# A decode block with cached attention: from the ninth K tile on, K loads move one V tile ahead, and value products, output weights and gather move half a step back

## The chip, the cores and the metric

The kernel runs on one NeuronCore of a Trainium2 chip. The metric is device microseconds of one execution. Of three runs of the kernel before, the median is 398.58 us (398.21 to 400.56). The profile is one further execution of the same program.

## The reference: what is computed

Eight tokens (B = 8, one per sequence, D = 512) go through an attention part and an MLP part, each behind a layer norm that is modulated by a conditioning vector `c`. All is float32. Cut to what matters:

```python
mod = (silu(c) @ w_mod).reshape(8, 6, 1, 512)          # sa, ca, ga, sb, cb, gb
h = layernorm(x) * (1 + ca) + sa
q = (h @ wq)                                            # 32 query heads of 128, 8 KV heads
k, v = k_cache[:, :, -2048:], v_cache[:, :, -2048:]     # of 8192 cached positions
o = softmax(q @ k.T * 128 ** -0.5) @ v
x = x + ga * (o @ wo)                                   # wo: 4096 x 512
h = layernorm(x) * (1 + cb) + sb
x = x + gb * (square(relu(h @ w1 + b1)) @ w2 + b2)      # 512 -> 1792 -> 512
```

For 8 sequences and 8 KV heads a window of 2048 positions by 128 numbers is read from the K cache and from the V cache, 67 MB each. Each number is used for four query heads only, so the kernel is a stream of 165 MB from HBM, with transposes and small matmuls beside it.

## The kernel before, in words

**Tiles.** A K tile K0 to K15 is one KV head for four of the sequences, 4 MiB, loaded as [128 partitions, 8192 numbers]. Two K tiles make one KV head (called a group here, g or `hk`, 0 to 7). A V tile V0 to V31 is one KV head for two sequences, 2 MiB; four V tiles make one group. K tiles lie in two "big" slots of SBUF, V tiles and other weights in five "small" slots (lines 19 and 20). The output weights `wo` come in three 2 MiB pieces, wo0 to wo2, each for two groups, in small slots; the piece for the last two groups comes with a part of `w1` into a big slot (called the tail load), the rest of `w1` into a small slot, and `w2` into the other big slot.

**Loads.** The list `loads` (lines 143 to 152) is a fixed order. `pump` (line 155) issues from its front as long as a slot of the right size is free in the order of the program; `done` (line 160) gives a slot back and calls `pump`. All loads go through SyncE's queue (SP) from lines 108 and 113, in the order of the list: where a load has to wait until PE has read the slot's last tile, everything behind it on SP waits too. The transfers then run one after another on the 16 DMA engines.

**Steps.** The work on TensorE is a loop of 38 steps, `s` (lines 500 to 539), in the order in which it is written (`manual_schedule`). A step takes half a K tile. Its parts are:

- `transposes` (line 220): 128x128 transposes of K on PE into PSUM (L231), copied out by ACT and DVE (L233); four calls a step. The last call of a K tile gives its slot back.
- `scores` (line 346): four matmuls of 512 columns (L357), two calls a step.
- `weighted(v, h)` (line 440): the value product of half a V tile, four matmuls of 512 columns (L449). Half 0 opens a PSUM tile and half 1 closes it; half 1 gives the V slot back, and four DVE operations (L463, L465) reduce the PSUM tile into `o_sb`. V tile v stands in step v + PV_LAG, where PV_LAG = 5: five steps behind the K tile's half with the same number.
- once a group, the softmax: `soft_a` (copy of the scores by ACT, L367, row maximum by DVE, L369), `soft_b` (transpose of the maxima, L374, and their maximum over the parts of a row, L377 and L383), `soft_c` (back into a column, L394 and L398, the exponential on ACT, L401, a copy by DVE, L409), `soft_d` (eight transposes of the probabilities, L425, two masked copies by DVE into `pT`, L428, and one matmul for the sums, L434).
- once a group, `gather` (line 469: one matmul, L473, and DVE's L477 and L478) and `project_o` (line 483: four matmuls with `wo`, L489, which give the `wo` slot back after each second group).

In the kernel before, both halves of V tile v stand in step v + 5, half 0 in the middle and half 1 at the end; `gather` stands in the middle of a group's second step ahead of `soft_d`, and `project_o` at the end of that step, behind `weighted(v, 1)`. In the table T is a transposes call, S a scores call, W a value product:

| step | PE's order before |
|---|---|
| first of a group | T S T W(v,0) T S [L374] T W(v,1) |
| second of a group | [L394] T S T gather soft_d W(v,0) T S T W(v,1) project_o |

After the last K tile (step 32 on) only the softmax of group 7, the last V tiles, the last `gather` and `project_o` remain, and then the MLP: `w1` (L594) and `w2` (L613), each behind a short chain on DVE. `spin` (L547) fills waits of PE with matmuls that nobody reads.

Of the kernel before, what the change touches and what calls it, by code (L numbers as in the profile page):

```python
# [20 lines left out]
def tile_adaln_cached_attention_mlp(  # L21
# [16 lines left out]
    B, HKV, SK, DH = k_cache.shape  # L38
# [9 lines left out]
    C = B // 2  # L48
    N = HKV * C
# [88 lines left out]
    def slot(key, n, o=0):  # L138

        t = slots[size_of(key)][held[key]][:, o:]  # L140
        return t[:, : t.shape[1] // n * n].rearrange("p (a n) -> p a n", n=n)

    loads = [("K", 0), *(("mod", k) for k in range(NQ)), *(("wq", k) for k in range(NQ)), ("K", 1), ("V", 0), ("K", 2)]
    for q in range(2, N // 2 + 2):
        if q > 2 and q < N // 2:
            loads.append(("K", q))
        for v in (2 * q - 4, 2 * q - 3):
            if v % (2 * C) == 2 * C - 4 and v < 6 * C:
                loads.append(("wo", v // (2 * C)))
            if v:  # L150
                loads.append(("V", v))
    loads += [("b", 0), ("tail", 0), ("w1", 0), ("w2", 0)]
    at = [0]

# [5 lines left out]
    def done(*keys):  # L160
        for k in keys:
            free[size_of(k)].append(held.pop(k))
        pump()
# [50 lines left out]
    odd = ident.rearrange("p (r u) -> p u r", u=2)  # L214
# [7 lines left out]
    def transposes(q, g, e):  # L222

        k = slot(("K", q), DH)
        if e == 0:
            KTS[q, g] = ktp.tile([P, 4, 16, 32], F32, name="kT")
        t = KTS[q, g]
        for a in range(2):
            p = ps_kt.tile([P, 4, P], F32, name="kt_ps")
            for i in range(4):  # L230
                nc.tensor.transpose(p[:, i, :], k[:, 32 * e + 16 * a + 4 * g + i, :], ident)  # L231
            i = 8 * e + 4 * a
            (nc.vector.tensor_copy if a else nc.scalar.copy)(  # L233
                t[:, :, i : i + 4, :], p.rearrange("p i (r u) -> p u i r", u=4)
            )
        if g == 3 and e == 1:
            done(("K", q))
# [89 lines left out]
    def turn_q(r):  # L327
        qs = work.tile([P, 512], F32, name="qs", tag="a", bufs=1)
        nc.scalar.copy(qs, pqs[r])
        pT_ = ps_m.tile([P, 512], F32, name="m_ps", tag="m_ps")  # L330
        for t in range(REP):
            nc.tensor.transpose(pT_[:, t * P : (t + 1) * P], qs[:, t * P : (t + 1) * P], ident)  # L332
        nc.vector.tensor_copy(  # L333
            qall[:, 4 * r : 4 * r + 4].rearrange("p g b t -> p t g b"),
            pT_.rearrange("p (t g b) -> p t g b", t=REP, g=4)[:, :, :, :B],
        )
# [28 lines left out]
    def soft_a(hk):  # L365
        ss = work.tile([P, 512], F32, name="ss", tag="a", bufs=1)
        nc.scalar.copy(ss, s_ps[0])  # L367
        mx = work.tile([P, 1], F32, name="mx")
        nc.vector.tensor_reduce(mx, ss, axis=AX.X, op=ALU.max)  # L369
        SS_[hk], MX_[hk] = ss, mx  # L370
# [21 lines left out]
    def soft_c(hk):  # L392
        pm = ps_m.tile([P, 512], F32, name="m_ps", tag="m_ps")
        nc.tensor.matmul(  # L394
            pm[:, 0:1], MX_.pop(hk).rearrange("p j r -> p (j r)"), ones[0:1, 0:1], start=True, stop=True
        )
        nm = work.tile([P, 1], F32, name="nm")
        nc.vector.tensor_copy(nm, pm[:, 0:1])  # L398
        pr = work.tile([P, 8, H, 2], F32, name="pr", bufs=1)
        z = work.tile([P, 1], F32, name="z")  # L400
        nc.scalar.activation(  # L401
            pr.rearrange("p i (r e) u -> p e i r u", e=2)[:, :, :, :, 0],
            SS_.pop(hk).rearrange("p (e i r) -> p e i r", e=2, i=8),
            AF.Exp,
            bias=nm,
            scale=SCALE,
            accum_out=z,
        )
        nc.vector.tensor_copy(pr[:, :, :, 1], pr[:, :, :, 0])  # L409
        zs = work.tile([P, B], F32, name="zs")  # L410
        nc.vector.tensor_scalar(zs, bq, z, None, op0=ALU.mult)
        P_[hk], RZP_[hk] = pr, zs
        if hk == HKV - 1:

            warm = work.tile([P, 1], F32, name="warm")
            nc.scalar.activation(warm, eps, AF.Sqrt)
# [23 lines left out]
    def weighted(n, h):  # L440

        hk, c = divmod(n, C)
        v = slot(("V", n), DH)
        if h == 0:
            O_[n] = ps_o.tile([P, 4, P], F32, name="o_ps")
        o = O_[n]
        for g in range(4):
            j = 16 * h + 4 * g
            nc.tensor.matmul(  # L449
                o[32 * g : 32 * g + 32].rearrange("p j d -> p (j d)"),  # L450
                PT_[hk][:, h, 4 * c + g].rearrange("p i r -> p (i r)"),
                v[:, j : j + 4, :].rearrange("p j d -> p (j d)"),
                start=(h == 0),
                stop=(h == 1),
            )
        if h == 0:
            return
        del O_[n]
        done(("V", n))
        if c == 0:  # L460
            OS_[hk] = work.tile([P, C, P], F32, name="o_sb", bufs=1)
        d = OS_[hk][:, c, :]
        nc.vector.tensor_scalar(d, o[:, 0, :], diag[:, 0:1], None, op0=ALU.mult)  # L463
        for j in range(1, 4):
            nc.vector.scalar_tensor_tensor(  # L465
                d, o[:, j, :], diag[:, j : j + 1], d, op0=ALU.mult, op1=ALU.add
            )

    def gather(hk):

        o = OS_.pop(hk)
        pp = ps_m.tile([P, 512], F32, name="m_ps", tag="m_ps")
        nc.tensor.matmul(  # L473
            pp, pick.rearrange("p t u -> p (t u)"), o.rearrange("p c d -> p (c d)"), start=True, stop=True
        )
        tr = work.tile([P, C, 4, 32], F32, name="tr", tag="b", bufs=1)
        nc.vector.transpose(tr, pp.rearrange("p (c d i) -> p c i d", c=C, i=4))  # L477
        nc.vector.tensor_mul(  # L478
            oT[hk % 2][:, :, :B].rearrange("p i (u c) -> p c i u", u=2),
            tr[:, :, :, :2],  # L480
            RZ_[hk].rearrange("p (u c) -> p c u", u=2)[:, :, None, :].to_broadcast([P, C, 4, 2]),
        )

    def project_o(hk):

        last = hk // 2 == HKV // 2 - 1
        w = slot(("tail", 0) if last else ("wo", hk // 2), D)
        for i in range(4):
            nc.tensor.matmul(  # L489
                wo_ps[32 * i : 32 * i + 32, :],  # L490
                oT[hk % 2][:, i, :],
                w[:, 4 * (hk % 2) + i, :],
                start=(hk == 0),
                stop=(hk == HKV - 1),
            )
        if hk % 2 and not last:
            done(("wo", hk // 2))


    for s in range(N + PV_LAG + 1):  # L500
        g, i = divmod(s, C)
        q, h = divmod(s, 2)
        v = s - PV_LAG
        soft = 1 <= g <= HKV
        if s == 1:
            turn_q(1)
        if i == 1 and soft:
            soft_c(g - 1)
        if s < N and (q, 2 * h) not in EARLY:
            transposes(q, 2 * h, 0)  # L510
        if 1 <= s <= N:
            scores((s - 1) // 2, 2 * ((s - 1) % 2) + 1)
            if i == 0:
                soft_a(g - 1)
        if s < N and (q, 2 * h) not in EARLY:
            transposes(q, 2 * h, 1)
        if v >= C and v % C == 0:
            gather(v // C - 1)
        if i == 1 and soft:
            soft_d(g - 1)  # L520
        if 0 <= v < N:
            weighted(v, 0)
        if s < N and (q, 2 * h + 1) not in EARLY:
            transposes(q, 2 * h + 1, 0)
        if s < N:
            scores(q, 2 * h)
        if s == 0:
            transposes(0, 3, 0)
            transposes(0, 3, 1)
        if i == 0 and soft:  # L530
            soft_b(g - 1)
        if s < N and (q, 2 * h + 1) not in EARLY:
            transposes(q, 2 * h + 1, 1)
        if 0 <= v < N:
            weighted(v, 1)
        if v >= C and v % C == 0:

            for hk in {N - C: (), N: (HKV - 2, HKV - 1)}.get(v, (v // C - 1,)):
                project_o(hk)


    spin_ps = ps_kt.tile([P, 4, P], F32, name="kt_ps")
# [117 lines left out]
```

## Time and profile before

| | |
|---|---|
| median of 3 runs | 398.58 us (398.21 to 400.56) |
| the profiled execution's own time | 401.07 us |
| its span, first to last instruction | 399.3 us |
| mean granted TensorE clock | 0.965 |
| HBM read | 164.77 MB, 413 GB/s over the span |
| busy | PE 334.1 us, DVE 178.5 us, ACT 97.4 us |
| K tile from issue to landing, median | 22.5 us |
| V tile from issue to landing, median | 24.9 us |

A group of the profile names line, engine, operation and `out<-in` with the tiles' names in the program; `big` and `small` are the slots. PE is the matmul side of TensorE, PEld its weight loads, SPq SyncE's queue. An idle time in square brackets stands ahead of an instruction, with what ended it. Times in a timeline or a chain are microseconds from the span's start.

### The profile page before, as it was taken

How to read it: one execution, taken by the hardware profiler on the slowest of the kernel's cores; microseconds unless marked ns; L12 is line 12 of the kernel's file. 1: busy time of each engine (PE TensorE's matmuls, PEld its weight loads, DVE VectorE, ACT ScalarE, POOL GpSimd, SP SyncE). 2: the span in 40 equal slices, each digit the busy share in tenths (PEclk: the TensorE clock that was granted, in tenths of full speed). 3: DMA queues.
4: the chain of work that ended last, by engine and by line, in shares of the span. 5: the costliest groups of instructions: out<-in, count | busy, mean ns of one | idle time of the engine just before them, and what ended most of it. 6: DMA issues, size and time to landing. Idle time of an engine off the chain costs nothing.

```text
span 399.3 us, 5987 instructions
## 1 busy us (share of the span) xinstructions
PE 334.1 (84%) x2550; PEld 165.0 (41%) x2550; DVE 178.5 (45%) x416; ACT 97.4 (24%) x169; POOL 2.5 (1%) x12
## 2 busy tenths in 40 slices
PE   1674589879998897899987988998879898997896
PEld 1430135454544443445542544454434454443124
DVE  6231024444555353644553445545552555455532
ACT  2210023342232222222321233122312222222010
POOL 2000000000000000000000000000000000000000
PEclk9996899999999998999999999999998999997899
DMA  8999999999999999999999999999999999999990
GB/s 328 418 436 428 446 416 427 435 420 442 408 430 437 435 419 432 433 418 430 422 450 410 437 422 442 415 437 415 441 414 442 418 438 420 423 428 406 433 376 26
DMA packets 10363, 165.22 MB, mean 414 GB/s; under 512 B 1112, under 2 KB 1376, under 8 KB 1632
## 3 DMA queue, kind: packets, MB, share of 16 engines
q1 hardware_dynamic: 10192, 164.71, 97.0%
q8 instruction: 20, 0.33, 0.3%
q10 hardware_dynamic: 144, 0.13, 0.1%
q14 instruction: 7, 0.06, 0.0%
HBM read 164.77 MB, written 0.07 MB: 413 GB/s over the span
## 4 chain that ended last, share of the span: by engine, by line
PE 49%; DMA 37%; DVE 9%; ACT 4%; issue 1%; SPq 0%; ACTq 0%; DVEq 0%
DMA big<-in_A_k_cache_dram 27%; PE kt_ps L231 19%; PE o_ps L449 11%; PE s_ps L357 9%; DMA small<-in_A_wq_dram 6%; DMA small<-in_w_mod_dram 4%; ACT pr L401 2%; DVE o_sb L465 2%; PE m_ps L473 2%; DVE kT L233 2%; DVE tr L477 1%; PE kt_ps L547 1%; PE m_ps L293 1%; DVE pT L428 1%; DVE pr L409 1%
## 5 line engine op out<-in xcount | busy, mean ns | idle before, releaser
L231 PE MATMUL kt_ps<-ident,big 128*128 128x128 f32 x1024 | 146.0, 285 | 30.7 <-DMA big<-in_A_k_cache_dram 20.0
L231 PEld LDWEIGHTS kt_ps<-ident,big 128*128 128x128 f32 x1024 | 112.7, 144 | 126.7 <-ACT kT L233 79.7
L233 DVE COPY kT<-kt_ps 128x512 f32<-128x512 f32 x128 | 88.3, 690 | 133.9 <-PE kt_ps L231 133.9
L233 ACT COPY kT<-kt_ps 128x512 f32<-128x512 f32 x128 | 75.0, 586 | 209.4 <-PE kt_ps L231 206.8
L357 PE MATMUL s_ps<-kT,qwin 128*32 128x512 f32 x512 | 70.1, 622 | 0.8 <-DVE qwin L343 0.8
L449 PE MATMUL o_ps<-small,pT 128*32 128x512 f32 x512 | 69.1, 620 | 0.0
L465 DVE SCALAR_TENSOR_TENSOR o_sb<-o_ps,diag,o_sb 128x128 f32<-128x128 f32 x96 | 33.7, 351 | 3.4
L318 PE MATMUL m_ps<-small,h1T 128*32 128x512 f32 x64 | 11.1, 829 | 10.3 <-DMA small<-in_A_wq_dram 10.3
L449 PEld LDWEIGHTS o_ps<-small,pT 128*32 128x32 f32 x512 | 11.4, 110 | 14.8 <-issue 13.9
L463 DVE TENSOR_SCALAR o_sb<-o_ps,diag 128x128 f32<-128x128 f32 x32 | 11.2, 351 | 13.9 <-PE o_ps L449 13.9
L357 PEld LDWEIGHTS s_ps<-kT,qwin 128*32 128x32 f32 x512 | 10.3, 109 | 12.8 <-issue 11.0
L401 ACT ACTIVATE pr<-ss,nm 128x512 f32<-128x512 f32 x8 | 9.7, 1219 | 19.1 <-DVE nm L398 19.1
L425 PE MATMUL m_ps<-ident,pr 128*128 128x128 f32 x64 | 10.5, 297 | 2.9 <-DVE tr L477 2.2
L425 PEld LDWEIGHTS m_ps<-ident,pr 128*128 128x128 f32 x64 | 7.9, 150 | 8.3 <-DVE tr L477 3.7
L473 PE MATMUL m_ps<-o_sb,pick 128*128 128x512 f32 x16 | 8.4, 604 | 3.1 <-DVE o_sb L465 1.6
L428 DVE TENSOR_TENSOR pT<-m_ps,mine 128x512 f32<-128x512 f32 x16 | 10.4, 686 | 0.4 <-PE m_ps L425 0.4
L333 DVE COPY qall<-m_ps 128x128 f32<-128x128 f32 x2 | 0.8, 390 | 21.4 <-PE m_ps L332 21.4
L318 PEld LDWEIGHTS m_ps<-small,h1T 128*32 128x32 f32 x64 | 2.1, 134 | 18.9 <-DMA small<-in_A_wq_dram 9.8
L409 DVE COPY pr<-pr 128x512 f32<-128x512 f32 x8 | 3.4, 428 | 12.1 <-ACT pr L401 12.1
L369 DVE TENSOR_REDUCE mx<-ss 128x1 f32<-128x512 f32 x8 | 5.5, 688 | 6.4 <-ACT ss L367 6.4
L293 PE MATMUL m_ps<-small,cT 128*32 128x512 f32 (+1 forms) x64 | 6.0, 492 | 2.0 <-DMA small<-in_w_mod_dram 2.0
L270 PE MATMUL m_ps<-xsum,sel 128*128 128x1 f32 x2 | 0.6, 362 | 7.9 <-DVE xsum L268 7.9
(123 smaller groups left out, 106.0 us busy)
## 6 DMA issues: line engine op xcount, KB each, us to landing
big<-in_A_k_cache_dram SPq DMA_DIRECT2D x16, 4096.0 KB, 22.5
small<-in_A_v_cache_dram SPq DMA_DIRECT2D x32, 2048.0 KB, 24.9
small<-in_A_wq_dram SPq DMA_DIRECT2D x4, 2048.0 KB, 22.2
small<-in_w_mod_dram SPq DMA_DIRECT2D x4, 1536.0 KB, 17.2
small<-in_A_wo_dram SPq DMA_DIRECT2D x3, 2048.0 KB, 21.1
big<-in_A_wo_dram SPq DMA_DIRECT2D x2, 1024.0 KB, 13.6
big<-in_B_w_dram SPq DMA_DIRECT2D x1, 2048.0 KB, 23.4
big<-in_B_w_dram SPq DMA_DIRECT2D x1, 1792.0 KB, 18.4
```

The source lines that it names most:

```text
L231: nc.tensor.transpose(p[:, i, :], k[:, 32 * e + 16 * a + 4 * g + i, :], ident)
L233: (nc.vector.tensor_copy if a else nc.scalar.copy)(t[:, :, i : i + 4, :], p.rearrange("p i (r u) -> p u i r", u=4))
L293: nc.tensor.matmul(pm[32 * q : 32 * q + 32, : (m1 - m0) * P].rearrange("p (m n) -> p m n", n=P), cT[:, kc, :], wv[:, m0:m1, q, :], start=( ...
L318: nc.tensor.matmul(pqs[r][32 * g : 32 * g + 32, :], hT[:, kc, :], w[:, 4 * r + g, :], start=(kc == 0), stop=(kc == NQ - 1),)
L357: nc.tensor.matmul(s_ps[0][32 * u : 32 * u + 32, :], qwin[hk % 2][:, 4 * c + u, o : o + 32], kT[:, u].rearrange("p i r -> p (i r)"), start ...
L401: nc.scalar.activation(pr.rearrange("p i (r e) u -> p e i r u", e=2)[:, :, :, :, 0], SS_.pop(hk).rearrange("p (e i r) -> p e i r", e=2, i= ...
L425: nc.tensor.transpose(pp[:, i * P : (i + 1) * P], pr[:, 4 * a + i].rearrange("p r u -> p (r u)"), ident)
L428: nc.vector.tensor_mul(PT_[hk][:, a].rearrange("p x i r -> p i x r"), pp.rearrange("p (i x r) -> p i x r", i=4, r=2 * REP), mine.rearrange ...
L449: nc.tensor.matmul(o[32 * g : 32 * g + 32].rearrange("p j d -> p (j d)"), PT_[hk][:, h, 4 * c + g].rearrange("p i r -> p (i r)"), v[:, j : ...
L463: nc.vector.tensor_scalar(d, o[:, 0, :], diag[:, 0:1], None, op0=ALU.mult)
L465: nc.vector.scalar_tensor_tensor(d, o[:, j, :], diag[:, j : j + 1], d, op0=ALU.mult, op1=ALU.add)
L473: nc.tensor.matmul(pp, pick.rearrange("p t u -> p (t u)"), o.rearrange("p c d -> p (c d)"), start=True, stop=True)
```

## The change

**The load list.** Up to V12 the list is as before. From K9 on each K tile stands one V tile further ahead: before, two V tiles lay between K8 and K9 behind wo1, now one. The list from K8 on:

```
before: K8 wo1 V12 V13 K9 V14 V15 K10 V16 V17 K11 V18 V19 K12 wo2 V20 V21 K13 V22 V23 K14 V24 V25 K15 V26 V27 ... V31
now:    K8 wo1 V12 K9 V13 V14 K10 V15 V16 K11 V17 V18 K12 V19 wo2 V20 K13 V21 V22 K14 V23 V24 K15 V25 V26 V27 ... V31
```

**The steps.** In every step, from the first V tile on, half 0 of V tile v moves from the middle to the end of its step, and half 1 from the end to the middle of the next step. `gather` moves to the end of a group's second step, `project_o` to the middle of the third. `soft_d` now stands behind the last half of the group before it, with no `gather` ahead of it. The last two `project_o` stand behind the loop, as they did in effect.

| step | PE's order now |
|---|---|
| first of a group | T S T W(v-1,1) T S [L374] T W(v,0) |
| second of a group | [L394] T S T W(v-1,1) soft_d T S T gather W(v,0) |
| third of a group | T S T project_o W(v-1,1) T S T W(v,0) |

```diff
-    for q in range(2, N // 2 + 2):
-        if q > 2 and q < N // 2:
+    late = N // 4
+    for v in range(1, N):
+
+        q, odd = divmod(v + 4 if v <= 2 * late - 4 else v + 5, 2)
+        if not odd and 2 < q < N // 2:
             loads.append(("K", q))
-        for v in (2 * q - 4, 2 * q - 3):
-            if v % (2 * C) == 2 * C - 4 and v < 6 * C:
-                loads.append(("wo", v // (2 * C)))
-            if v:
-                loads.append(("V", v))
+        if v % (2 * C) == 2 * C - 4 and v < 6 * C:
+            loads.append(("wo", v // (2 * C)))
+        loads.append(("V", v))
...
+        ends = v >= C and v % C == 0
...
-        if v >= C and v % C == 0:
-            gather(v // C - 1)
+        if v > C and v % C == 1 and v < N - C:
+            project_o(v // C - 1)
+        if 1 <= v <= N:
+            weighted(v - 1, 1)
         if i == 1 and soft:
             soft_d(g - 1)
-        if 0 <= v < N:
-            weighted(v, 0)
...
+        if ends:
+            gather(v // C - 1)
         if 0 <= v < N:
-            weighted(v, 1)
-        if v >= C and v % C == 0:
-
-            for hk in {N - C: (), N: (HKV - 2, HKV - 1)}.get(v, (v // C - 1,)):
-                project_o(hk)
+            weighted(v, 0)
+
+    project_o(HKV - 2)
+    project_o(HKV - 1)
```

How this moves the instructions is shown at three places. SyncE's queue, from K13 to V25; `big_91` and `big_92` are the two K slots, the other tiles are small slots. Before:

```order
L108 DMA big_92<-in_A_k_cache_dram 128x1x8192
L108 DMA small_93<-in_A_v_cache_dram 128x1x4096
L108 DMA small_94<-in_A_v_cache_dram 128x1x4096
L108 DMA big_91<-in_A_k_cache_dram 128x1x8192
L108 DMA small_96<-in_A_v_cache_dram 128x1x4096
L108 DMA small_97<-in_A_v_cache_dram 128x1x4096
L108 DMA big_92<-in_A_k_cache_dram 128x1x8192
```

Now:

```order
L108 DMA big_92<-in_A_k_cache_dram 128x1x8192
L108 DMA small_97<-in_A_v_cache_dram 128x1x4096
L108 DMA small_93<-in_A_v_cache_dram 128x1x4096
L108 DMA big_91<-in_A_k_cache_dram 128x1x8192
L108 DMA small_94<-in_A_v_cache_dram 128x1x4096
L108 DMA small_96<-in_A_v_cache_dram 128x1x4096
L108 DMA big_92<-in_A_k_cache_dram 128x1x8192
L108 DMA small_97<-in_A_v_cache_dram 128x1x4096
```

Before, the rows are K13, V22, V23, K14, V24, V25, K15; now K13, V21, V22, K14, V23, V24, K15, V25. Each K tile has moved up by one row, and the V tile that stood just ahead of it stands just behind it.

PE after the last transpose of K (the end of the loop, group 7's softmax), where `o_ps` are value products, `m_ps<-ident,mx`, `m_ps<-ones,mrow` and `m_ps<-ident,pr` the softmax's, and `m_ps<-o_sb,pick` is `gather`. Before:

```order
L357 MATMUL s_ps<-kT,qwin_116 32x512 x4
L449 MATMUL o_ps<-small_94,pT 32x512 x4
L374 MATMUL m_ps<-ident,mx 1x128
L449 MATMUL o_ps<-small_94,pT 32x512 x4
L394 MATMUL m_ps<-ones,mrow 128x1
L473 MATMUL m_ps<-o_sb,pick 128x512
L425 MATMUL m_ps<-ident,pr 128x128 x8
L434 MATMUL m_ps<-zs,tsel 128x8
L449 MATMUL o_ps<-small_96,pT 32x512 x8
```

Now:

```order
L358 MATMUL s_ps<-kT,qwin_116 32x512 x4
L450 MATMUL o_ps<-small_93,pT 32x512 x4
L375 MATMUL m_ps<-ident,mx 1x128
L450 MATMUL o_ps<-small_94,pT 32x512 x4
L395 MATMUL m_ps<-ones,mrow 128x1
L450 MATMUL o_ps<-small_94,pT 32x512 x4
L426 MATMUL m_ps<-ident,pr 128x128 x8
L435 MATMUL m_ps<-zs,tsel 128x8
L474 MATMUL m_ps<-o_sb,pick 128x512
L450 MATMUL o_ps<-small_95,pT 32x512 x8
```

One more value product (half 1 of V26) stands behind the last scores, and `gather` of group 6 has moved from ahead of the probabilities' transposes to behind the sums.

DVE at the same place; `mx`, `m_`, `mrow`, `nm`, `pr`, `zs` and `pT` are the softmax's, `o_sb` rows reduce a value product. Before:

```order
L369 TENSOR_REDUCE mx<-ss 128x1
L377 TENSOR_REDUCE m_2892<-m_ps 1x32
L383 TENSOR_SCALAR mrow<-m_2892 1x128
L463 TENSOR_SCALAR o_sb<-o_ps,diag 128x128
L465 SCALAR_TENSOR_TENSOR o_sb<-o_ps,diag,o_sb 128x128 x3
L398 COPY nm<-m_ps 128x1
L409 COPY pr<-pr 128x512
L411 TENSOR_SCALAR zs<-bq,z 128x8
L477 STREAM_TRANSPOSE tr<-m_ps 128x512
L478 TENSOR_TENSOR oT_135<-tr,rz 128x4x4x2
L428 TENSOR_TENSOR pT<-m_ps,mine 128x4x16x8 x2
```

Now:

```order
L370 TENSOR_REDUCE mx<-ss 128x1
L464 TENSOR_SCALAR o_sb<-o_ps,diag 128x128
L466 SCALAR_TENSOR_TENSOR o_sb<-o_ps,diag,o_sb 128x128 x3
L378 TENSOR_REDUCE m_2887<-m_ps 1x32
L384 TENSOR_SCALAR mrow<-m_2887 1x128
L399 COPY nm<-m_ps 128x1
L410 COPY pr<-pr 128x512
L412 TENSOR_SCALAR zs<-bq,z 128x8
L464 TENSOR_SCALAR o_sb<-o_ps,diag 128x128
L466 SCALAR_TENSOR_TENSOR o_sb<-o_ps,diag,o_sb 128x128 x3
L429 TENSOR_TENSOR pT<-m_ps,mine 128x4x16x8 x2
L439 RECIPROCAL rz<-m_ps 128x8
```

The reduction of a value product that stood ahead of `nm` stands ahead of `m_` now, a second one stands between `zs` and `pT`, and `gather`'s two operations are gone from ahead of `pT`. In the changed kernel the functions' lines are one higher, and the lines behind the loop four higher.

## The prediction
> **What bounds the kernel now.** I read the page first, for the busy shares and the time from issue to landing.
>
> ```profile
> span 399.3 us, 5987 instructions
> PE 334.1 (84%) x2550; PEld 165.0 (41%) x2550; DVE 178.5 (45%) x416; ACT 97.4 (24%) x169; POOL 2.5 (1%) x12
> big<-in_A_k_cache_dram SPq DMA_DIRECT2D x16, 4096.0 KB, 22.5
> small<-in_A_v_cache_dram SPq DMA_DIRECT2D x32, 2048.0 KB, 24.9
> ```
>
> PE is busy 84%, the other engines half or less. Then the table by stages, for the DMA engines: it gives length, busy times, PE's clock, DMA share and GB/s.
>
> ```profile
> 250.00:300.00 50.00, 44.06 (x339) 21.94 (x337) 25.77 (x56) 12.16 (x21) 0.00 (x0) 1.00 1.00 425
> 300.00:350.00 50.00, 46.09 (x346) 23.54 (x347) 23.44 (x49) 13.37 (x23) 0.00 (x0) 0.97 1.00 428
> 387.00:388.00 1.00, 1.00 (x14) 0.28 (x2) 0.00 (x0) 0.00 (x0) 0.00 (x0) 1.00 0.75 291
> 391.00:391.50 0.50, 0.50 (x3) 0.20 (x2) 0.36 (x2) 0.00 (x0) 0.00 (x0) 1.00 0.05 16
> 391.50:392.00 0.50, 0.50 (x3) 0.26 (x2) 0.00 (x0) 0.00 (x0) 0.00 (x0) 1.00 0.00 0
> ```
>
> The transfers fill the 16 engines (share 1.00) until 387 us and have ended at 391.5. No order of the loads makes this stream shorter; it can only deliver what is needed sooner. So two chains run side by side, and the question is which ends last, and how much PE waits for the stream. PE's timeline shows the waits, in brackets:
>
> ```profile
> 216.78 1.07 PE L231 MATMUL kt_ps<-ident,big 128*128 128x128 f32 x8 [2.81 <-DMA big<-in_A_k_cache_dram]
> 236.28 1.06 PE L231 MATMUL kt_ps<-ident,big 128*128 128x128 f32 x8 [1.68 <-DMA big<-in_A_k_cache_dram]
> 275.81 1.07 PE L231 MATMUL kt_ps<-ident,big 128*128 128x128 f32 x8 [1.39 <-DMA big<-in_A_k_cache_dram]
> 300.26 1.94 PE L231 MATMUL kt_ps<-ident,big 128*128 128x128 f32 x8 [2.51 <-DMA big<-in_A_k_cache_dram]
> 316.81 1.06 PE L449 MATMUL o_ps<-small,pT 128*32 128x512 f32 x8
> 319.74 1.07 PE L231 MATMUL kt_ps<-ident,big 128*128 128x128 f32 x8 [1.86 <-DMA big<-in_A_k_cache_dram]
> 341.65 1.09 PE L231 MATMUL kt_ps<-ident,big 128*128 128x128 f32 x8
> ```
>
> These five (K9, K10, K12, K13, K14; together 2.81 + 1.68 + 1.39 + 2.51 + 1.86 = 10.25 us) are all waits for a K tile after 200 us. Behind K14 PE waits for no load again: it starts K15 at 341.65 with no bracket, and from 319.74 to the end the time is PE's own work and the softmax and MLP chains. The chain of waits (start, length, what) and the issues of single loads say when tiles land:
>
> ```profile
> 295.93 23.68 DMA big<-in_A_k_cache_dram
> L108 SPq DMA_DIRECT2D small<-in_A_v_cache_dram x1: 535/535/535, 284.2 to 284.2; - x1
> DMA to landing us min/median/max: 25.7/25.7/25.7
> L108 SPq DMA_DIRECT2D small<-in_A_v_cache_dram x1: 534/534/534, 274.5 to 274.5; - x1
> DMA to landing us min/median/max: 30.5/30.5/30.5
> ```
>
> K14 lands at 295.93 + 23.68 = 319.6, and PE starts on it at 319.74. V23 lands at 284.2 + 25.7 = 309.9, V22 at 274.5 + 30.5 = 305.0. Transfers are one behind another, so a V tile takes 4.9 us of the stream and a K tile 319.6 - 309.9 = 9.7. Last, the end of the kernel:
>
> ```profile
> 357.76 1.07 PE L357 MATMUL s_ps<-kT,qwin 128*32 128x512 f32 x8
> 358.88 0.59 ACT L367 COPY ss<-s_ps 128x512 f32<-128x512 f32 x1 [1.81 <-PE s_ps L357]
> 359.50 0.69 DVE L369 TENSOR_REDUCE mx<-ss 128x1 f32<-128x512 f32 x1
> 361.40 0.38 PE L394 MATMUL m_ps<-ones,mrow 1*128 1x1 f32 x2
> 361.59 0.35 DVE L463 TENSOR_SCALAR o_sb<-o_ps,diag 128x128 f32<-128x128 f32 x1 [0.41 <-PE o_ps L449]
> 361.97 1.12 DVE L465 SCALAR_TENSOR_TENSOR o_sb<-o_ps,diag,o_sb 128x128 f32<-128x128 f32 x3
> 363.01 0.15 DVE L398 COPY nm<-m_ps 128x1 f32<-128x1 f32 x1
> 363.26 1.21 ACT L401 ACTIVATE pr<-ss,nm 128x512 f32<-128x512 f32 x1 [3.79 <-DVE nm L398]
> 364.50 0.43 DVE L409 COPY pr<-pr 128x512 f32<-128x512 f32 x1 [1.34 <-ACT pr L401]
> 366.14 0.69 DVE L428 TENSOR_TENSOR pT<-m_ps,mine 128x512 f32<-128x512 f32 x1 [0.20 <-PE m_ps L425]
> 366.99 0.69 DVE L428 TENSOR_TENSOR pT<-m_ps,mine 128x512 f32<-128x512 f32 x1 [0.16 <-PE m_ps L425]
> 367.41 9.28 PE L449 MATMUL o_ps<-small,pT 128*32 128x512 f32 x64
> 392.87 3.27 PE L613 MATMUL m_ps<-big,rT 128*32 128x128 f32 x112
> ```
>
> The last scores (357.76), the softmax of group 7, the last four V tiles from 367.41, and, after `gather`, `project_o` and the MLP's chain, the matmuls with `w2` from 392.87 to 396.14. The last bytes of `w2` were there at 391.5: PE's chain ends last, by about 4 us.
>
> **The change, part by part.**
>
> *Loads.* The same bytes in another order: the stream still ends at 391.5. Each K tile from K9 on loses one V tile ahead of it, 4.9 us. Of K14: V23 goes behind it, so it lands at 319.6 - 4.9 = 314.7. PE must be ready by then. K13 lands at 300.1 - 4.9 = 295.2 (before, PE started on it at 300.26, as it landed); its work took until 316.81 + 1.06 = 317.87, which is 17.6 us, so PE is ready for K14 at 295.3 + 17.6 = 312.9 if K12 was done by 295.3. K12 lands 4.9 us earlier too, at 270.8, and took from 275.81 to 300.26 - 2.51 = 297.75, 21.9 us: done at 292.8. So PE starts K14 at 314.85, still by waiting for it (1.9 us), and K13 too (2.5 us). K9 and K10 are where PE no longer waits, or hardly: PE is ready for K9 at 216.78 - 2.81 = 213.97, and it lands at 211.7. The term is therefore not the 10.25 us of waits but the lead of the last waited-for tile: **-4.9 us** at K14. K15 lands at 314.7 + 4.9 + 4.9 + 9.7 = 334.2, and PE needs it at 341.65 - 4.9 = 336.7: no wait.
>
> *What the lead takes from the V tiles.* An odd V tile now lands behind the K tile, 9.7 us later: V23 at 314.7 + 4.9 = 319.6. Its first use is `weighted(23, 0)`, now the last piece of K14's first half: seven pieces of about 1 us and the maxima's 0.4 ahead of it, so at 314.85 + 7.4 = 322.3. It is 2.7 us early. In its old place, three pieces into the step, it would have come at 318 and held PE for 1.6 us; this is what the half step pays for, and why I cost the late V tiles at nothing. If this cover goes, each us costs one. V21 (behind K13) is early by 295.3 + 7.2 - 300.0 = 2.5, V25 by more.
>
> *Slots.* Half 1 now ends half a step, about 4 us, later, and with it every V slot's return. A V tile takes 24.9 us from issue to landing (median) of which 4.9 are its own: 20 us of queue stand ahead of it, 16 remain. The K tiles are tighter: SP is in order, and K14, which waits for K12's slot, holds V23 and V24 behind it. K14 was issued at 295.93; the transfer ahead of it is now V22, landing at 305.0, and no longer V23. 9.1 us remain, and K12 is done 4.9 us earlier. Cost nothing.
>
> *A group's second step.* Here PE's own pieces wait for the softmax:
>
> ```profile
> 331.51 1.43 PE L231 MATMUL kt_ps<-ident,big 128*128 128x128 f32 x8 [1.13 <-ACT kT L233]
> 334.61 0.66 PE L425 MATMUL m_ps<-ident,pr 128*128 128x128 f32 x4 [0.37 <-DVE tr L477]
> 335.44 0.39 PE L434 MATMUL m_ps<-zs,tsel 128*128 128x8 f32 x2 [0.17 <-DVE pT L428]
> ```
>
> The 1.13 us stand behind ACT, whose exponential waited for `nm`, which stood behind the reduction of a value product on DVE. That reduction is now half a step earlier: up to 1.1 us less. In exchange the last half of the old group stands ahead of `soft_d`, and its reduction (0.35 + 1.12 us) ahead of the `pT` copies, so the sums wait about 1.1 us and not 0.37 + 0.17. Between -1.1 and +0.6; I take **-0.4** for group 6, the one group whose second step lies behind K14's start. The other groups' second steps, and all that changes place before 200 us, stand ahead of a wait for a K tile, of which the list of waits has nine:
>
> ```profile
> PE kt_ps L231 <- DMA big<-in_A_k_cache_dram: 20.0, 9, 3.5
> ```
>
> What is gained or lost ahead of such a wait of 1 to 3.5 us changes the wait and not the start of the next tile.
>
> *The end.* `project_o` and a half product pass from K14's steps into K15's; up to the last scores PE's pieces are the same in number. Behind them stands one value product more, 1.06 us, beside the copy and the maximum (358.88 to 360.19); with that cover it costs nothing, without it 1 us. On DVE a reduction (0.35 + 1.12, with starts 1.50 us) moves from ahead of `nm` to ahead of the maximum of the maxima. `mx` ends at 360.19; plus 1.50 is 361.7; from there to `nm` lie 1.3 us (the two small operations, L394's 0.38 and the steps between), so 363.0, as before (363.01). No gain, no loss. The second reduction stands between `zs` (ends about 365.1) and `pT`: `pT`'s copies run from 366.6 to 368.0 instead of 366.14 to 367.68. Then `gather`, 1.1 us on PE, which before was hidden in the wait for the exponential, now needs the PSUM buffer that the second copy reads: 368.05 to 369.15, and the last V tiles queue behind it in order. They start at 369.15, not 367.41: **+1.7 us**. Bounds: +0.5 if gather finds a buffer and only the copies are later; +2.8 if the first reduction delays `nm` by another 1.1. The nearest rows speak for the middle.
>
> **Sum:** -4.9 - 0.4 + 1.7 = **-3.6 us**: a span of 395.7, against an own time of 401.07 some 397.5, and on the median of 398.58, which is without the profiler, **395.0 us**. The ends of the terms give -4.9 - 1.1 + 0.5 = -5.5 and -4.9 + 0.6 + 2.8 = -1.5. The first is cut by the stream: `w2`'s last bytes at 391.5, then the last fourteenth of the block of 3.27 us, 0.23, and its latency, some 0.5 in all, against 396.14 now: no more than -4.1. The forecast's own range is 394.2 to 397.1.
>
> **The clock** enters at the end:
>
> ```profile
> 299.86:303.27 3.41, 3.01 (x16) 1.77 (x16) 0.69 (x1) 0.59 (x1) 0.00 (x0) 0.50 0.99 423
> 364.71:371.54 6.83, 6.55 (x30) 3.03 (x34) 3.07 (x9) 1.26 (x2) 0.00 (x0) 0.50 1.00 420
> ```
>
> PE's granted clock was 0.50 for 3.41 us from the wait for K13 on, and for 6.83 us from 364.71, after the gaps of the last softmax. In the second stretch the value products ran at half speed from 367.41 to 371.54: half of 4.13 us, 2.1, was lost on the path. I leave this as it is in the forecast, since the gaps stay, and take it up in the rivals. [...]
>
> **The rivals.**
>
> 1. *The end meets the last weights.* The windows fall otherwise, or the extra value product in the softmax keeps the clock up: PE's chain gains up to 2 us more and then waits for `w2`: -4.1, 394.5 us. For it: PE has one piece more to do between the scores and the exponential. Against: the waits there stay as long.
> 2. *The end loses more*, by one more window of 3.41 us at half speed: +1.7, so -1.9 and 396.7 us. For it: gather and sums now wait behind each other just where the clock fell.
> 3. *The transfers bound it anyway*: no change, 398.6 us. For it: share 1.00 for 387 us. Against: 391.5 is 4 us ahead of 396.14. [...]
> 4. *Slower: the queue runs dry.* If PE gives K10's, K12's and K14's slots back over 9.1 us later than now, the engines stop, and with no slack in the stream each us dry is lost. At 12 us that is 3 x 2.9 = 8.7: the stream ends at 400.2, the span at 400.2 + 0.5 + 3.1 = 403.8, about 403 on the median. For it: slots return later and the lead has less queue ahead of it. Against: PE gets earlier, not later.
>
> **How the numbers follow.** Forecast 0.40, rival 1 0.25, rival 2 0.17, rival 3 0.10, rival 4 0.08. One per cent, about what a measurement of this kernel tells from no change, is 394.6 below and 402.6 above. Faster by more: two thirds of rival 1 and a third of the forecast's cases, 0.17 + 0.13 = 0.30. Slower by more: most of rival 4, 0.06. The rest, 0.64, is within. The range leaves out rival 4 and a tenth below, and has 0.3 more above rival 3 for the spread of the runs: 393.5 to 398.9.
>
> **What would show it.** In the changed profile: K14's wait ends near 314.9, its length about 1.9 us; K13 waits still, K9 and K10 hardly; no value product waits for a V tile; the DMA share stays 1.00 to 387; `w2`'s matmuls start near 389.3; the last V tiles' products start about 11.5 us after the last scores and not 367.41 - 357.76 = 9.65. Wrong: waits for V tiles at the end of steps, a DMA share below 1.00 in the middle, K14 starting later than 316, or `w2`'s matmuls waiting for a DMA, which would be rival 1.

## The result, and the profile after

| | before | after |
|---|---|---|
| median of 22 runs each | 400.00 us | 397.14 us |
| lowest and highest | 397.96 to 402.06 | 396.85 to 400.42 |
| ratio of the runs, 95% interval | | 0.9938 (0.9920 to 0.9957) |
| profiled execution, own time and span | 401.07, 399.3 | 397.39, 395.6 |

The change makes the kernel faster, by 0.6%. The forecast met the profiled execution (span 395.7 forecast, 395.6 measured) and missed the median: 395.0 forecast, 397.14 measured. The two kernels' runs are also spread differently: of the changed kernel's 22 runs 20 lie within 0.8 us (396.85 to 397.65), while those of the kernel before are strewn over 4 us.

PE's waits for K tiles after 190 us in the changed kernel's timeline (lines are one higher than before; the rows are K8, K10, K12, K13, then `project_o` of group 5, K14, and K15, which starts without a wait):

```profile
192.68 1.06 PE L232 MATMUL kt_ps<-ident,big 128*128 128x128 f32 x8 [1.68 <-DMA big<-in_A_k_cache_dram]
231.66 1.07 PE L232 MATMUL kt_ps<-ident,big 128*128 128x128 f32 x8 [1.47 <-DMA big<-in_A_k_cache_dram]
270.65 1.07 PE L232 MATMUL kt_ps<-ident,big 128*128 128x128 f32 x8 [1.47 <-DMA big<-in_A_k_cache_dram]
295.11 1.94 PE L232 MATMUL kt_ps<-ident,big 128*128 128x128 f32 x8 [3.96 <-DMA big<-in_A_k_cache_dram]
299.69 1.07 PE L490 MATMUL wo_ps<-small,oT 128*32 128x512 f32 x8
314.62 1.06 PE L232 MATMUL kt_ps<-ident,big 128*128 128x128 f32 x8 [0.89 <-DMA big<-in_A_k_cache_dram]
335.05 1.09 PE L232 MATMUL kt_ps<-ident,big 128*128 128x128 f32 x8
```

K14 starts at 314.62 and not at 319.74: 5.1 us sooner. There are still waits: what has changed is when the tile lands. The end of the kernel, from the last scores:

```profile
352.02 1.07 PE L358 MATMUL s_ps<-kT,qwin 128*32 128x512 f32 x8
356.76 0.16 DVE L399 COPY nm<-m_ps 128x1 f32<-128x1 f32 x1 [0.47 <-PE m_ps L395]
358.85 1.06 PE L426 MATMUL m_ps<-ident,pr 128*128 128x128 f32 x8 [1.12 <-DVE zs L412]
360.90 0.39 PE L435 MATMUL m_ps<-zs,tsel 128*128 128x8 f32 x2 [0.99 <-DVE pT L429]
361.50 1.12 PE L474 MATMUL m_ps<-o_sb,pick 128*128 128x512 f32 x2 [0.21 <-DVE pT L429]
362.56 5.53 PE L450 MATMUL o_ps<-small,pT 128*32 128x512 f32 x48
369.94 1.92 PE L450 MATMUL o_ps<-small,pT 128*32 128x512 f32 x16 [1.85 <-DMA small<-in_A_v_cache_dram]
388.38 1.95 PE L617 MATMUL m_ps<-big,rT 128*32 128x128 f32 x64
390.73 1.72 PE L617 MATMUL m_ps<-big,rT 128*32 128x128 f32 x48 [0.39 <-DMA big<-in_B_w_dram]
```

The last scores come 5.74 us sooner than before (357.76). Then PE waits 1.85 us for V31, the last V tile, and 0.39 us for a piece of `w2`. Neither wait was there before; the one for `w2` ends last, so in this execution the stream of loads sets the end. The stream itself, in the table by stages (busy times, clock, DMA share, GB/s in the last columns):

```profile
300.00:350.00 50.00, 47.78 (x376) 23.63 (x368) 26.73 (x58) 13.97 (x24) 0.00 (x0) 1.00 1.01 428
387.00:388.00 1.00, 1.00 (x3) 0.20 (x2) 0.00 (x0) 0.00 (x0) 0.00 (x0) 1.00 0.62 256
390.00:391.00 1.00, 0.61 (x26) 0.34 (x20) 0.00 (x0) 0.00 (x0) 0.00 (x0) 1.00 0.20 76
```

It runs much as it did: the share is 1.01 at 380 to 385 us and 0.97 at 385 to 386 (before: 0.96 and 0.98), then it falls, to 0.00 from 392 on, where it was 0.00 from 391.5 before.

### The profile page after: what moved, and what is told of

Same layout as the page of the kernel before. It is cut to its first block, busy times and chain, and to the rows that moved or that the text cites. A ratio compares the mean times of both kernels' runs of the same rounds, so it can differ in the third digit from the quotient of the medians.

```text
span 395.6 us, 5981 instructions
## 1 busy us (share of the span) xinstructions
PE 330.5 (84%) x2550; PEld 162.4 (41%) x2550; DVE 178.2 (45%) x416; ACT 97.5 (25%) x169; POOL 2.4 (1%) x12
## 4 chain that ended last, share of the span: by engine, by line
DMA 46%; PE 42%; DVE 7%; ACT 4%; issue 1%; ACTq 0%; DVEq 0%
DMA big<-in_A_k_cache_dram 31%; PE kt_ps L232 20%; PE s_ps L358 9%; PE o_ps L450 7%; DMA small<-in_A_wq_dram 6%; DMA big<-in_B_w_dram 5%; DMA small<-in_A_v_cache_dram 4%; ACT pr L402 2%; DVE o_sb L466 2%; DVE kT L234 2%; PE m_ps L294 1%; ACT kT L234 1%; DVE pT L429 1%; PE m_ps L319 1%; DVE pr L410 1%
## 5 line engine op out<-in xcount | busy, mean ns | idle before, releaser
L358 PE MATMUL s_ps<-kT,qwin 128*32 128x512 f32 x512 | 69.2, 614 | 0.8 <-DVE qwin L344 0.8
L450 PE MATMUL o_ps<-small,pT 128*32 128x512 f32 x512 | 67.1, 602 | 1.9 <-DMA small<-in_A_v_cache_dram 1.9
L435 PE MATMUL m_ps<-zs,tsel 128*128 128x8 f32 x16 | 3.1, 266 | 8.7 <-DVE pT L429 8.7
L426 PEld LDWEIGHTS m_ps<-ident,pr 128*128 128x128 f32 x64 | 6.9, 141 | 7.0 <-issue 7.0
L426 PE MATMUL m_ps<-ident,pr 128*128 128x128 f32 x64 | 8.7, 278 | 1.1 <-DVE zs L412 1.1
```

What stands on the lines that cost most here:

```text
L358: nc.tensor.matmul(s_ps[0][32 * u : 32 * u + 32, :], qwin[hk % 2][:, 4 * c + u, o : o + 32], kT[:, u].rearrange("p i r -> p (i r)"), start ...
L426: nc.tensor.transpose(pp[:, i * P : (i + 1) * P], pr[:, 4 * a + i].rearrange("p r u -> p (r u)"), ident)
L450: nc.tensor.matmul(o[32 * g : 32 * g + 32].rearrange("p j d -> p (j d)"), PT_[hk][:, h, 4 * c + g].rearrange("p i r -> p (i r)"), v[:, j : ...
```

## The experiments

Theory A, formed from the two traces: the kernel before ends with TensorE's own chain, whose length depends on where half-speed windows of its clock (stretches of 3.4 us for which the profile shows a granted clock of 0.50, as from 299.86 to 303.27 us in the kernel before) fall in that run; the changed kernel ends with the stream, which is the same in every run. Theory B, the rival: both end with TensorE's chain, the change shifts it by a constant, and the spread is the chip's. Beside these stood the question which part of the change does it. Each kernel was timed beside the kernel before on one chip:

| kernel | runs | median (lowest to highest) | before | ratio, 95% interval |
|---|---|---|---|---|
| kernel before, again | 12 | 399.12 (398.03 to 402.07) | 399.70 | 0.9974 (0.9942 to 1.0006) |
| before, half of V28 left out | 10 | 399.77 (398.25 to 401.87) | 399.70 | 0.9995 (0.9967 to 1.0023) |
| after, half of V28 left out | 10 | 395.20 (394.67 to 400.38) | 399.70 | 0.9899 (0.9861 to 0.9937) |
| loads alone | 10 | 397.40 (397.12 to 397.74) | 399.70 | 0.9937 (0.9914 to 0.9960) |
| steps alone | 10 | 401.16 (398.94 to 401.97) | 399.50 | 1.0031 (1.0005 to 1.0056) |
| before, one idle pair | 12 | 400.30 (397.87 to 403.31) | 399.50 | 1.0007 (0.9973 to 1.0040) |
| after, one idle pair | 10 | 397.16 (396.99 to 398.00) | 399.50 | 0.9932 (0.9908 to 0.9956) |
| K14 and K15 alone moved ahead | 10 | 397.30 (397.01 to 399.38) | 399.85 | 0.9944 (0.9916 to 0.9972) |
| K9 to K13 alone moved ahead | 10 | 400.70 (399.80 to 402.91) | 399.85 | 1.0022 (0.9996 to 1.0048) |
| changed kernel, again | 10 | 397.33 (396.89 to 400.63) | 399.85 | 0.9958 (0.9926 to 0.9990) |
| before, four idle pairs | 12 | 398.24 (398.00 to 398.66) | 399.85 | 0.9948 (0.9925 to 0.9971) |
| loads alone, three idle pairs | 12 | 397.22 (396.87 to 399.77) | 399.43 | 0.9956 (0.9935 to 0.9977) |

### What sets the end

The kernel before, unchanged:

> The kernel before once more, for its spread and its clock run by run. Theory A (the kernel before ends with TensorE's own chain, and TensorE's half-speed windows fall differently in each run; the changed kernel ends with the stream of loads, whose end is the same in each run): times spread over 398 to 402 us, median near 400, ratio 1.000, and none below 397.0, the stream's end plus what lies behind it; in the profile no wait of a value product for V31. Theory B (both kernels end with TensorE's chain, the change shifts it by a constant, the spread is the chip's): the changed kernel should show the same spread of 4 us, and here too the ratio is 1.000.

Time and mean granted clock go together over its 12 runs (correlation -0.83): the fastest, 398.03 us, had 0.974, the slowest, 402.07 us, 0.957. Over the 35 runs of the kernel before in the same session, which reach from 398.20 to 405.00 us, it is -0.73. The profile taken here is of the slowest run:

```profile
321.38 1.71 PE L231 MATMUL kt_ps<-ident,big 128*128 128x128 f32 x8 [3.31 <-DMA big<-in_A_k_cache_dram]
```

```profile
321.60:325.00 3.40, 3.40 (x17) 1.41 (x16) 0.69 (x1) 0.59 (x1) 0.00 (x0) 0.51 1.03 439
366.00:369.40 3.40, 2.94 (x7) 1.35 (x8) 1.77 (x6) 2.69 (x4) 0.00 (x0) 0.50 0.95 403
```

Half-speed windows (0.51 and 0.50) stand behind K14's wait and in the last softmax, both behind the last wait for a load, where nothing takes them up.

Half of V28's bytes left out, in either kernel. The same edit loads V31 in one piece, where both kernels load it in two halves:

```diff
-            for x in range(2 if key == ("V", N * 2 - 1) else 1):
-                cols = slice(x * NJ * DH // 2, (x + 1) * NJ * DH // 2) if key == ("V", N * 2 - 1) else slice(None)
-                nc.sync.dma_start(t[:, cols], v[..., cols])
+            cols = slice(0, NJ * DH // 2) if key == ("V", 28) else slice(None)
+            nc.sync.dma_start(t[:, cols], v[..., cols])
```

> Leaves out half of V28's bytes (1 MiB, 2.4 us of the stream, behind K15 and ahead of V31). Theory A: nobody waits for V31 or the MLP's weights in the kernel before, so no change: ratio 0.998 to 1.002, span 399. If the stream bound the kernel before as well: 2.4 us less, ratio 0.994.

> The changed kernel, without half of V28's bytes (1 MiB, 2.4 us). Theory A: V31 and w2 land 2.4 us earlier, TensorE's wait of 1.85 us for V31 goes, and its own chain ends the kernel again: 1.9 us below the changed kernel, about 395.2 in its good runs, and the spread of 2 to 4 us comes back; ratio to the kernel before 0.988 to 0.991. Theory B: as the changed kernel, 397.1, ratio 0.994.

The kernel before did not move (0.9995): its end does not hang on the stream. The changed kernel fell from 397.1 to 395.2, as Theory A has it, and not all of the 2.4 us came. In its profile the wait for V31 is gone and `w2` is no longer waited for:

```profile
363.07 7.98 PE L449 MATMUL o_ps<-small,pT 128*32 128x512 f32 x64
387.22 3.26 PE L616 MATMUL m_ps<-big,rT 128*32 128x128 f32 x112
```

All 64 matmuls of the last V tiles and all 112 of `w2` run in one piece. So in its good runs the changed kernel ends with the stream, and Theory B, which expected 397.1, falls. These ten runs lie from 394.67 to 400.38, and time goes with the clock (-0.81). That the spread came back is not shown by this, as the changed kernel itself gave 396.89 to 400.63 when run again (below).

### Which part of the change does it

Loads alone is the kernel before with the new list; steps alone is the changed kernel with the old list. Their first lines, in this order:

```diff
-    for q in range(2, N // 2 + 2):
-        if q > 2 and q < N // 2:
...
+    late = N // 4
+    for v in range(1, N):
+        q, odd = divmod(v + 4 if v <= 2 * late - 4 else v + 5, 2)
...
```

```diff
-    late = N // 4
-    for v in range(1, N):
...
+    for q in range(2, N // 2 + 2):
+        if q > 2 and q < N // 2:
...
```

> The new order of loads with the old order of steps. My account: K14 starts 4.9 us earlier, but half 0 of each odd V tile behind a K tile, three pieces into the step, waits about 1.6 us for its landing; that wait is paid once behind K14's start (V23; V25 is in time), so 4.9 - 1.6 = 3.3 us are left, no loss in the last softmax: span 396, ratio 0.992 to 0.996. If the lead needs the half step: 0.998 to 1.005. If the half step is not needed: as the whole change, 0.994, without any wait for V tiles in the loop.

> The old order of loads with the new order of steps. My account: K14 lands and starts where it did (319.7), the group's second step saves 0.6 us, the last softmax loses 0.9 us: ratio 0.998 to 1.003. If the half step itself were the gain: 0.994. Theory A says nothing else here than that the end is TensorE's: no wait for V31.

The new order of loads is the whole gain: 397.40, ratio 0.9937. The waits for late V tiles that the half step was to cover are there; PE's timeline of this kernel has V15, V19, V21, K14 and V23:

```profile
236.38 1.06 PE L450 MATMUL o_ps<-small,pT 128*32 128x512 f32 x8 [1.72 <-DMA small<-in_A_v_cache_dram]
275.40 1.06 PE L450 MATMUL o_ps<-small,pT 128*32 128x512 f32 x8 [0.86 <-DMA small<-in_A_v_cache_dram]
299.84 1.06 PE L450 MATMUL o_ps<-small,pT 128*32 128x512 f32 x8 [1.71 <-DMA small<-in_A_v_cache_dram]
314.55 1.06 PE L232 MATMUL kt_ps<-ident,big 128*128 128x128 f32 x8 [1.52 <-DMA big<-in_A_k_cache_dram]
319.36 1.06 PE L450 MATMUL o_ps<-small,pT 128*32 128x512 f32 x8 [1.73 <-DMA small<-in_A_v_cache_dram]
```

The 1.73 us at V23 (forecast: 1.6) stand behind the last wait for K and push TensorE's chain back, but it has that much to spare against the stream. The half step buys time that nobody needs. Steps alone is slower by 0.3%, with its interval just above 1. Its profile has K13, `project_o` of group 5, K14, the last scores and the last four V tiles at:

```profile
299.78 1.94 PE L231 MATMUL kt_ps<-ident,big 128*128 128x128 f32 x8 [3.96 <-DMA big<-in_A_k_cache_dram]
305.23 1.07 PE L489 MATMUL wo_ps<-small,oT 128*32 128x512 f32 x8
319.28 1.06 PE L231 MATMUL kt_ps<-ident,big 128*128 128x128 f32 x8
356.67 1.06 PE L357 MATMUL s_ps<-kT,qwin 128*32 128x512 f32 x8
367.92 8.18 PE L449 MATMUL o_ps<-small,pT 128*32 128x512 f32 x64
```

K13's wait is 3.96 us, where the kernel before had 2.51, mainly as `project_o` (1.07 us) stands behind K13's landing now and not ahead of it. That is not where the time goes in this execution: K14 starts without a wait at 319.28, no later than before (319.74). The end is longer: from the last scores to the last V tiles it takes 11.25 us, where the kernel before took 9.65. There was half speed there in both: in the kernel before the clock was 0.50 for 6.83 us from 364.71 on, and here, by the rows, `gather` took 1.84 us (1.12 in the changed kernel) and the 64 matmuls of the last V tiles 8.18 (7.25 in the kernel with four pairs). That this is the 0.3% is argued from one profile, not shown.

### Which tile's lead counts

The kernel before, with some K tiles moved ahead of one V tile; the second kernel has `range(9, 14)` here:

```diff
+    for q in range(14, 16):
+        n = loads.index(("K", q))
+        loads[n - 1 : n + 1] = loads[n], loads[n - 1]
     loads += [("b", 0), ("tail", 0), ("w1", 0), ("w2", 0)]
```

> The kernel before with only K14 and K15 moved ahead of one V tile. K14 lands near 314.5, but TensorE is not ready before 317.9, since K12 and K13 come when they did: K14's wait (1.9 to 3.3 us in the profiles of the kernel before) is all that goes, V23 is there in time. Lead account: 1.9 to 3.3 us less, median 396.9 to 397.8 where the kernel before has 399.7, ratio 0.992 to 0.996. If only the lead of the last tile counted, whatever TensorE's state: 5 us, cut by the stream at 397.1.

> The kernel before with K9 to K13 moved ahead of one V tile and K14, K15 in their old places. Lead account: TensorE is ready for K14 at 313 and waits 6 us for it, until 319.6 as before; everything earlier is given back in that one wait: ratio 0.999 to 1.005. If each wait removed counted for itself (2.8 + 1.7 + 1.4 us and more): ratio 0.985 to 0.993.

With K9 to K13 alone nothing is gained (1.0022), and PE's timeline shows where it goes, at K14:

```profile
320.19 1.94 PE L234 MATMUL kt_ps<-ident,big 128*128 128x128 f32 x8 [6.41 <-DMA big<-in_A_k_cache_dram]
```

One wait of 6.41 us gives back all that the five tiles won. With K14 and K15 alone almost all of the gain is there (397.30). The wait for K14 is gone, that for K13 has stayed:

```profile
300.33 1.06 PE L234 MATMUL kt_ps<-ident,big 128*128 128x128 f32 x8 [2.53 <-DMA big<-in_A_k_cache_dram]
319.75 1.07 PE L452 MATMUL o_ps<-small,pT 128*32 128x512 f32 x8 [0.17 <-DMA small<-in_A_v_cache_dram]
390.53 1.72 PE L616 MATMUL m_ps<-big,rT 128*32 128x128 f32 x48 [0.39 <-DMA big<-in_B_w_dram]
```

The rows are K13, V23 and `w2`: the removal of one wait of about 2 us is enough to reach the stream's end. The median does not tell the two accounts of this kernel apart, since both allow 397.1; the profile does. K14 starts without a wait at 316.47, when TensorE is through with K13:

```profile
316.47 1.09 PE L234 MATMUL kt_ps<-ident,big 128*128 128x128 f32 x8
```

It had landed by some 314.9, an estimate: 4.9 us, one V tile, ahead of V23 at 319.75. So TensorE's own state did limit the lead. Four of its ten runs lie at 398.7 to 399.4, with the clock at 0.957 to 0.965, where loads alone had none; that it has less to spare than the whole list is argued.

### Where the spread comes from

One pair of matmuls that nobody reads, ahead of `gather` in the kernel before and ahead of `soft_d` in the changed one:

```diff
+        if s == N + 1:
+            spin(1)
         if v >= C and v % C == 0:
             gather(v // C - 1)
```

The kernel with four pairs has these as well:

```diff
+        if s == N - 4:
+            spin(2)
         if s < N and (q, 2 * h) not in EARLY:
             transposes(q, 2 * h, 0)
...
+        if s == N + 1:
+            spin(1)
         if i == 1 and soft:
             soft_d(g - 1)
```

> The kernel before with one idle matmul pair (1 us, nobody reads it) in TensorE's longest gap of the last softmax, between L394 and gather, which was 1.46 us. Theory A: the clock stays up more often behind it, the last value products run at full speed, up to 2 us less in the runs that lost them: median 398 to 399.5 where the kernel before has 400, ratio 0.994 to 0.998, fewer runs above 400. If the spread does not come from there: 1.000 to 1.002, same spread.

> The changed kernel with one idle matmul pair (1 us) in the gap of 1.12 us ahead of the probabilities' transposes of the last softmax. Theory A: it ends with the stream, so the median stays at 397.1 (ratio 0.993 to 0.995); at most the few runs at 399 to 400 get rarer. Theory B: the same gain as in the kernel before, up to 2 us more, ratio 0.989 to 0.991.

> The kernel before with idle matmuls that nobody reads: two pairs (2 us) ahead of K14, in the wait of 1.9 to 3.3 us, and one pair on either side of gather in the last softmax (gaps of 1.46 and 0.65 us). If the half-speed windows behind K14's wait and in the last softmax make the spread: median 398 to 399, most runs within 1 us, ratio 0.995 to 0.998. If they do not, or the windows do not look at such matmuls: 1.000 to 1.003 and the spread of 4 us stays, as with one pair alone (1.0007).

One pair in the longest gap of the last softmax did nothing for the time (1.0007, 397.87 to 403.31): that expectation failed. In its one profile the rows of the last softmax are those of the full clock (the 64 matmuls of the last V tiles take 7.25 us, as in the kernel with four pairs), and two half-speed windows stand behind K14's wait, by an estimate from the rows: three groups of eight matmuls there take 1.94, 1.94 and 1.97 us where they take 1.06 to 1.09 elsewhere. Two pairs in K14's wait as well, and one more in the softmax, brought the runs together: 398.00 to 398.66, with 399.85 beside it. In the profile the clock is full where it had been halved:

```profile
317.75 1.98 PE L505 MATMUL kt_ps<-ident 128*128 128x512 f32 x4
319.72 1.06 PE L231 MATMUL kt_ps<-ident,big 128*128 128x128 f32 x8
```

```profile
319.00:323.00 4.00, 4.00 (x30) 2.03 (x32) 1.58 (x4) 1.73 (x3) 0.00 (x0) 1.00 1.01 430
363.00:370.00 7.00, 6.50 (x46) 2.75 (x46) 3.91 (x12) 2.70 (x4) 0.00 (x0) 1.00 1.00 421
```

So, by these runs (0.66 us between 12 of them, where 35 of the kernel before lie within 4.71), the half-speed windows in these two places together make most of the spread. The profiles agree with that. A window of 3.4 us at half speed costs 1.7 us, an estimate: half its length. The executions with none, one and two of them behind K14's wait took 398.51 us (four pairs), 400.02 (half of V28 left out, which did not move the median) and 401.07, 401.70 and 402.07 (the kernel before, with one pair, and again). The one with one window has it right behind K14's wait, where eight transposes take 1.94 us in place of 1.06:

```profile
319.59 1.94 PE L230 MATMUL kt_ps<-ident,big 128*128 128x128 f32 x8 [3.28 <-DMA big<-in_A_k_cache_dram]
```

That the runs of the kernel before at 398 are those without such windows follows from this, but none of the profiles is of such a run. How much each place adds over many runs was not separated. In the changed kernel an idle pair moved nothing (397.16), as the stream sets its end.

The changed kernel again, and a last version, loads alone with one pair ahead of K14 and one on either side of `gather`:

> The changed kernel once more, beside these on one chip. Theory A: 396.9 to 397.5, no tie of time and clock, ratio 0.992 to 0.996; and the same as the new order of loads alone (397.4).

> The new order of loads with the old order of steps, and idle matmuls that nobody reads: one pair ahead of K14 (wait 1.5 us) and one pair on either side of gather in the last softmax. Theory A: the stream's end stays the bound, median 397.0 to 397.4, and since neither V tiles nor half-speed windows push TensorE's chain past it, all runs lie within 1 us, where the changed kernel has a tenth to a third of its runs at 399 to 400.6; ratio 0.992 to 0.996. It cannot go below 397.0 less 0.2.

Both medians lie at the stream's end. The changed kernel had three of ten runs at 399.8 to 400.6 here, and over them time and clock go together (-0.73), which I had not expected. The profile of a good run, 396.89 us, has about two half-speed windows in the last softmax, some 358.6 to 365.4 us by an estimate from its rows: eight transposes take 1.90 us (1.06 in the first profile of this kernel), `gather` 2.08 (1.12), the last 64 matmuls 8.31 in one piece. It still waits for `w2`, by 0.22 us: that much the changed kernel takes up. What the slow three lost beyond it is open. The last version was to hold all its runs within 1 us; three of twelve came at 398.5 to 399.8. What these lost is open as well, since its one profile is of a good run. No version that reads all bytes has a median below the changed kernel's 397.14.

## Why the prediction was right and wrong

- *The stream ends where it did.* Right to within half a us (392 and 391.5). Left out of the forecast was that V31, too, would be waited for (1.85 us). The list of what the stream can cut named `w2` alone.
- *K14 lands and starts 4.9 us sooner.* Right: 314.62, forecast 314.85. That the term is the lead at the last waited-for tile and not the sum of the waits is what the two kernels with single tiles moved show. The waits' lengths were off: K13 3.96 where 2.5 was forecast, K14 0.89 where 1.9 was. The forecast kept K13's work at 17.6 us and let `project_o` pass from K14's steps into K15's only; it passes from K12's into K13's as well (the row at 299.69). So TensorE came to K13 earlier and took 18.6 us for it (295.11 to 313.73). The start of K14 did not depend on it, as there was a wait left.
- *Late V tiles cost nothing.* Right for the changed kernel: no value product ahead of V31's waits; and 1.73 us was the price in the old place, forecast 1.6. That "this is what the half step pays for" is wrong: without it the kernel is as fast.
- *The group's second step, -0.4.* From K14's start to the last scores it was 38.02 us before (357.76 - 319.74) and is 37.40 now (352.02 - 314.62): -0.6.
- *The end, +1.7.* From the last scores to the last four V tiles it was 9.65 and is 10.54 us: +0.9. `gather` stands on the path as forecast (361.50, 1.12 us). But `nm` comes 4.74 us after the scores' start instead of 5.25, and the half speed that the kernel before had here (clock 0.50 for 6.83 us from 364.71 on) is not in this profile (1.00 at 352 to 376 us).
- *The clock.* The first rival's case came: no half-speed window in the last softmax of this profile (clock 1.00), and the end meets the loads. The forecast named `w2`'s matmuls waiting for a DMA as the sign of that rival, and they wait (0.39 us). So it is luck that the forecast's -3.6 meets the -3.7 of the profiled execution (401.07 to 397.39). Up to the last four V tiles TensorE was ahead by 4.85 us (367.41 to 362.56) and not by 3.6. Those V tiles then took 9.30 us (362.56 to 371.86) where they had taken 9.28, since the full clock's gain (9.28 to 5.53 + 1.92 = 7.45) went into the wait for V31 (1.85), and 1.1 us more were lost up to the end of `w2`'s matmuls.
- *The sum's bounds.* The lower end of "the forecast's own range", 394.2, does not come out of its terms: 398.58 less the bound of 4.1 is 394.5. Of the 0.5 us behind the last bytes in that bound, 0.23 are the last fourteenth's; the rest, a latency, was an estimate that no run shows by itself. In the changed kernel's profile the last matmuls of `w2` end at 392.45 (390.73 + 1.72), with the last bytes before 392.
- *The step that failed* is the sum's last one, "on the median of 398.58, which is without the profiler, 395.0 us". It took the 2.5 us between the profiled execution and the median of three runs for the profiler's cost, and took the same 3.6 us off both. The profiler's cost was a term without a row. No such cost shows: the profiled executions of the changed kernel and of the kernel with four pairs took 397.39 and 398.51 us, and their medians are 397.14 and 398.24. Each run's own time is about 1.8 us above its span, in the profiled one (401.07 and 399.3) as in the changed kernel's (397.39 and 395.6). The 401.07 was one draw from 398 to 402, and 398.58 a lucky median, since 22 runs give 400.00. The gain is not a constant that can be taken off any run: it is the distance from that run to the stream's end at 397.0, which is 4 us from 401.07 but 1.6 us from 398.58. In the forecast's sum TensorE's own chain still ends the kernel, 0.5 us later than the stream alone would; in the runs the stream ends it, as leaving out half of V28 showed (395.20). The working had this bound ("no more than -4.1") and held it against one execution only. Done right, the forecast is 401.07 - 4.1 = 397.0 for every run that is not held up. The medians moved by 2.9 us (400.00 to 397.14).
- *The chances.* Within 1% was given 0.64, and 0.6% is within. But 1% was also taken for what a measurement can tell from no change, and this one tells 0.6% (0.9920 to 0.9957): it has 22 runs of each kernel, and the changed kernel's lie close together.

## What to carry to other kernels

Where two chains end within a few us of each other, forecast the time at which each ends and take the later one, run by run; a gain worked out on one profiled execution must not be taken off a median. In a loop that waits for loads again and again, as here, only the last wait's end counts, and a lead on the earlier tiles is given back there: here moving two of seven tiles gave nearly all of it (397.30 us, all seven 397.40), and moving the other five gave nothing (400.70). And before work is moved about to cover a wait, ask whether the engine that would wait still sets the end: the half step covered 1.7 us that the stream had made free.

## What the runs showed of the hardware

Between executions of the kernel before and its variants, one half-speed window of 3.4 us behind the last wait for a load went with 1.5 us, and two with 2.6 to 3.6 us (400.02, and 401.07 to 402.07, where 398.51 had none). Of two waits of the same length one brought such a window and the other did not: the kernel before had a clock of 0.50 from 299.86 to 303.27, from its wait of 2.51 us for K13 on, and the kernel with K14 and K15 moved ahead kept 1.00 behind one of 2.53 us at the same place. The table by stages of that kernel behind its wait:

```profile
300.30:303.70 3.40, 3.37 (x28) 2.03 (x32) 0.93 (x2) 1.17 (x2) 0.00 (x0) 1.00 1.06 453
```

One pair of idle matmuls in one gap did not help (ratio 1.0007); four pairs, over the last wait and the last softmax, brought 12 runs to within 0.66 us. And the 16 DMA engines are not all busy to the end of the stream. Their mean share in the changed kernel was 0.62 at 387 to 388 us and 0.20 at 390 to 391, with the last bytes before 392; in the kernel before it was 1.00 at 300 to 350 us, 0.75 at 387 to 388 and 0.05 at 391 to 391.5.
